# A decode step of cached attention and a gated feed-forward block: the TensorE program as a loop over four units

## The chip, the cores and the metric

The kernel runs on one core of a Trainium2 chip. The metric is the device time of one execution in microseconds (us); lower is better. Engines are called PE (TensorE), DVE (VectorE), ACT (ScalarE), POOL (GpSimd) and SP (SyncE, which here only issues DMAs).

## What is computed

One decode step for a batch of two, all in bfloat16 with D = 448:

```python
xn = layernorm(x)                                    # x: (2, 1, 448)
q = (xn @ wq).reshape(2, 1, 16, 256)                 # wq: (448, 4096)
k, v = last 2048 of 8192 cache positions, 8 heads    # each serves two query heads
o = softmax(q k^T / 16) v                            # per batch and head
s = o.reshape(2, 1, 4096) @ wo                       # wo: (4096, 448)
g = silu(relu(xn @ w1) @ w2)                         # w1: (448, 1792), w2: (1792, 448)
out = x + s * g
```

## The kernel before

The K and V that are read make 33.5 MB of the 44.1 MB that the kernel reads. They are cut into four units u = 0 to 3, each with one batch and four key heads (`divmod(u, 2)`), so that a unit's K or V is one tile of 128 partitions by 16384 values (32 KB in a partition, 4 MB in all). A load of such a tile is one DMA.

For each unit the work is a chain:

- `do_turn(u)`: DVE transposes the K tile in four pieces from a buffer `ub` into the one tile `kt`.
- `do_S(u)`: PE makes the scores in the PSUM bank `sbk`: four matmuls with `amask`, one for each column group (`tile_position`), that put a large negative number where a query does not belong to a key head, and then 32 matmuls with `qz`, the spread out queries.
- `do_chain(u)`: DVE takes the maximum `rm`, PE turns it into a row of `mbk`, DVE folds it into `m8` and `mrow`, PE turns it back (a float32 matmul with `one_f`), DVE copies it to `bias`, ACT computes the exponential `e_sb`, DVE transposes it into `ptd`, PE sorts it into the bank `pbk` with 16 matmuls, and ACT copies it into `pt[u % 2]`. `do_sum(u)` makes the reciprocal `rs` of the sum (PE `gsum`, DVE).
- `do_PV(u)`: 32 matmuls of `pt` with the V tile into `obk`.
- `do_o(u)`: DVE scales to `o_sb`, PE transposes it with four matmuls, DVE spreads it into `at_exp`.

The queries come first: `do_q_mm` multiplies the normalised x (`xr`) with wq, which lies in the tile `wqo` on 128 partitions as seven slots of half rows, into `obk`; `do_q` scales (`q_n`), transposes (`q_t`), spreads with four matmuls (`rep4`) and makes all eight pieces of `qz`. The feed-forward block is `do_H` (28 matmuls with w1 into `hbk`), `do_hT` and `do_F` (56 matmuls with w2 into `fbk`, then silu). At the end 128 matmuls with wo into the bank `wbk`, a product with g, a sum with x, and the store.

Buffers: `ub` has three tiles, and `place` says which load uses which: k0, k2 (after k0) and v2 in tile 0; k1, v1 and v3 in tile 1; v0 and k3 in tile 2. A K tile is free when its turn is over (`freed[f"k{u}"]`), a V tile when its `do_PV` is over. wo overwrites wq in `wqo`; w1 and w2 have tiles of their own.

`_Prog` records every operation with the operations that it depends on. Each engine gets its list in the order of recording; an operation that somebody needs counts up its engine's semaphore, every DMA has a semaphore of its own, and waits are for values of these counts. All of it is written out straight: no engine branches. All big loads are on SP, in the order wq (first slot), k0, wq (rest), k1, v0, k2, v1, k3, v2, w1, v3, w2, wo in four parts (`WO_PARTS`: 20, 8, 2 and 2 of its 32 slots), and then 15 small loads `probe` that nothing but SP's last wait needs. SP issues in order, so a load that waits for its buffer holds back the ones behind it. Matmuls have the helper's line L244 in the profile; loads have L36.

The order of PE in the second half of the recording:

```python
do_S(1); do_PV(0); do_o(0); do_chain(1); do_sum(1)
do_S(2); do_PV(1); do_chain(2); do_sum(2); do_o(1)
do_PV(2); do_S(3); do_H(); do_chain(3); do_sum(3); do_o(2)
do_PV(3); do_o(3)    # then the transposes of at_exp, do_F, wo
```

Of the kernel before, what the change touches and what calls it, by code (L numbers as in the profile page):

```python
# [5 lines left out]
BF = mybir.dt.bfloat16  # L6
# [8 lines left out]
class _Op:  # L15
    __slots__ = ("eng", "fn", "deps", "dma", "needed", "value", "sem")

    def __init__(self, eng, fn, deps, dma):
        self.eng, self.fn, self.deps, self.dma = eng, fn, deps, dma
        self.needed, self.value, self.sem = dma, 0, None  # L20


class _Prog:


    def __init__(self, nc, es):
        self.nc, self.es = nc, es
        self.lists = {PE: [], DVE: [], ACTE: [], SP: [], POOL: []}

    def op(self, eng, fn, deps=()):  # L30
        o = _Op(eng, fn, [d for d in deps if d is not None], False)
        self.lists[eng].append(o)
        return o

    def dma(self, eng, dst, src, deps=()):
        o = _Op(eng, lambda e: e.dma_start(dst, src), [d for d in deps if d is not None], True)  # L36
        self.lists[eng].append(o)
        return o

    def run(self):  # L40
        n = 0
        for ops in self.lists.values():
            for o in ops:
                for d in o.deps:
                    d.needed = True
        for e, ops in self.lists.items():
            sem, count = self.es.enter_context(self.nc.semaphore(f"s_{e}")), 0
            for o in ops:
                if o.dma:
                    n += 1  # L50
                    o.sem, o.value = self.es.enter_context(self.nc.semaphore(f"d_{n}")), 16
                elif o.needed:
                    count += 1
                    o.sem, o.value = sem, count

        def emit(eng, ops):
            seen = {}
            for o in ops:
                want = {}
                for d in o.deps:  # L60
                    if d.value > want.get(id(d.sem), (None, 0))[1]:
                        want[id(d.sem)] = (d.sem, d.value)
                for key, (sem, value) in want.items():
                    if value > seen.get(key, 0):
                        eng.wait_ge(sem, value)
                        seen[key] = value
                made = o.fn(eng) if o.fn else None
                if o.needed:
                    made.then_inc(o.sem, 16 if o.dma else 1)

        for name, e in (("sync", SP), ("scalar", ACTE), ("gpsimd", POOL), ("vector", DVE), ("tensor", PE)):
            emit(getattr(self.nc, name), self.lists[e])


def bass_recurrent_scan__sliding_block_cached__dense_activation_relu__decode_kernel(
# [25 lines left out]
    SLOTS = 7  # L101
    HC = HD // 2
    FC = DFF // 2
    WO_PARTS = [20, 8, 2, 2]
    NCOL = D // 4

    es = contextlib.ExitStack()
    with es:
# [5 lines left out]
        def psum(name, shape, dt):  # L114
            return es.enter_context(nc.psum_tensor(name, shape, dt))
# [7 lines left out]
        one_f = named("one_f", [128, 1], F32)  # L123
        par8 = named("par8", [128, 8], F32)
        par2 = named("par2", [128, 2], F32)
        qmask = named("qmask", [128, 4], F32)
        fold = named("fold", [128, 32], BF)
        gsum = named("gsum", [128, 128], F32)
        amask = named("amask", [128, 32], BF)
        x_sb = named("x_sb", [128, D], BF)  # L130
        xg = named("xg", [128, 9 * 128], BF)
# [4 lines left out]
        xr = named("xr", [128, SLOTS * 4], BF)  # L136
        q_n = named("q_n", [128, 512], BF)
        q_t = named("q_t", [128, 512], BF)
        rep4 = named("rep4", [128, 512], BF)
        m8 = named("m8", [1, 8], F32)  # L140
        qz = named("qz", [128, NU * 8 * 32], BF)
        fold8 = named("fold8", [128, 8], F32)
        xr2 = named("xr2", [128, SLOTS * 32], BF)
        h_n = named("h_n", [128, FC // 4], BF)
        h_t = named("h_t", [128, FC // 4], BF)
# [5 lines left out]
        probe = named("probe", [16, 16 * 15], BF)  # L151
        rm = named("rm", [128, 1], F32)
        mrow = named("mrow", [128, 128], F32)
# [5 lines left out]
        pt = [named(f"pt{i}", [128, 512], BF) for i in range(2)]  # L159
# [3 lines left out]
        wqo = named("wqo", [128, 32 * D], BF)  # L163
        assert SLOTS * HC <= 32 * D
        ub = [named(f"ub{i}", [128, UW], BF) for i in range(3)]
        kt = named("kt", [128, UW], BF)
        w1_sb = named("w1_sb", [128, SLOTS * FC], BF)
        w2_sb = named("w2_sb", [128, 14 * D], BF)

        sbk = psum("sbk", [128, 512], F32)  # L170
        pbk = psum("pbk", [128, 512], F32)
        obk = psum("obk", [128, 512], F32)
        fbk = psum("fbk", [128, 512], F32)
        wbk = psum("wbk", [128, 512], F32)
        mbk = psum("mbk", [128, 512], F32)
        hbk = psum("hbk", [128, 512], F32)

        def mbk_ap(lo, n, rows=128):
            return view(mbk, lo, [[1, n]], n=rows)

        def kv_src(u, cache):
            hg, b = divmod(u, 2)
            a = cache[b, 4 * hg:4 * hg + 4, SK - W:SK, :]
            return a.rearrange("h (p t) d -> p h (t d)", t=NT)
# [5 lines left out]

        wq_src = A_wq.rearrange("r (hf c) -> (r hf) c", hf=2).rearrange("(p s) c -> p (s c)", s=SLOTS)
        w1_src = B_w1.rearrange("r (hf c) -> (r hf) c", hf=2).rearrange("(p s) c -> p (s c)", s=SLOTS)
        w2_src = B_w2.rearrange("(hf p j) n -> p hf (j n)", hf=2, j=7)
# [5 lines left out]
            base=0, pattern=[[-1, 128]], channel_multiplier=1), [i0])  # L199
        i1 = pr.op(POOL, lambda e: e.memset(ident_f[:, :], 0.0), [p_id])  # L200
# [3 lines left out]
        p_one = pr.op(POOL, lambda e: e.memset(one_f[:, :], 1.0), [p_idf])  # L204
        p_at = pr.op(POOL, lambda e: e.memset(at2[:, :], 0.0))
        p_x2 = pr.op(POOL, lambda e: e.memset(xr2[:, :], 0.0))
# [7 lines left out]
        for e2 in range(2):  # L214
            v_xn = pr.op(DVE, lambda e, e2=e2: e.tensor_scalar(
                out=view(xg, 128 - 127 * e2, [[256, 4], [128, 2], [2, 64]], n=B),
                in0=view(x_sb, 3 * e2, [[1, 4], [0, 2], [SLOTS, 64]], n=B),
                scalar1=st2[0:B, 0:1], scalar2=rstd[0:B, 0:1],
                op0=ALU.subtract, op1=ALU.mult), [v_rs])
        v_par = pr.op(DVE, lambda e: e.tensor_reduce(  # L220
            out=par2[:, :], in_=view(ident, 0, [[1, 2], [2, 64]]), axis=AX.X, op=ALU.add), [p_id])
        v_par8 = pr.op(DVE, lambda e: e.tensor_copy(
            view(par8, 0, [[2, 4], [1, 2]]), view(par2, 0, [[0, 4], [1, 2]])), [v_par])
        v_qm = pr.op(DVE, lambda e: e.tensor_reduce(
            out=qmask[:, :], in_=view(ident, 0, [[32, 4], [1, 32]]), axis=AX.X, op=ALU.add))
# [5 lines left out]
        for i in range(4):  # L231
# [5 lines left out]
        v_gs = pr.op(DVE, lambda e: e.tensor_copy(  # L237
            view(gsum, 0, [[8, 16], [1, 8]]), view(fold8, 0, [[0, 16], [1, 8]])), [v_fold8])
        v_am = pr.op(DVE, lambda e: e.tensor_scalar(
            out=view(amask, 0, [[8, 4], [2, 4], [1, 2]]), in0=view(ident, 0, [[0, 4], [1, 4], [0, 2]]),  # L240
            scalar1=-1.0, scalar2=BIG, op0=ALU.add, op1=ALU.mult), [p_id])

# [4 lines left out]
        for s in range(SLOTS):  # L247
            m_xr = pr.op(PE, mm(mbk_ap(2 * s, 2), xg[0:B, 128 * s + 128:128 * s + 256], ident[0:B, 0:B], s == 0),
                         [v_xn, p_id])
        v_xr = pr.op(DVE, lambda e: e.tensor_tensor(  # L250
            out=view(xr, 0, [[4, SLOTS], [2, 2], [1, 2]]), in0=view(mbk, 0, [[2, SLOTS], [0, 2], [1, 2]]),
            in1=view(par8, 0, [[1, SLOTS], [1, 2], [0, 2]]), op=ALU.mult), [m_xr, v_par8])

        v_xr2 = pr.op(DVE, lambda e: e.tensor_copy(
            view(xr2, 0, [[32, SLOTS], [1, 2], [16, 2]]), view(xr, 0, [[4, SLOTS], [2, 2], [1, 2]])), [v_xr, p_x2])

        st = {"mbk": v_xr}
        dma_of, freed = {}, {}
        place = {"k0": 0, "k1": 1, "v0": 2, "k2": 0, "v1": 1, "k3": 2, "v2": 0, "v3": 1}
        last_in = {}  # L260

        def load(name):
            i, u = place[name], int(name[1])
            dma_of[name] = pr.dma(SP, ub[i][:, :], kv_src(u, A_k_cache if name[0] == "k" else A_v_cache),
                                  [freed.get(last_in.get(i))])
            last_in[i] = name

        def do_turn(u, g0=0, g1=4):
            src = ub[place[f"k{u}"]]
            s32, k32 = src[:, :].bitcast(F32), kt[:, :].bitcast(F32)  # L270
            for g in range(g0, g1):
                lo, hi = g * UW // 8, (g + 1) * UW // 8
                st["turn", u, g] = pr.op(DVE, lambda e, lo=lo, hi=hi: e.transpose(k32[:, lo:hi], s32[:, lo:hi]),  # L273
                                         [dma_of[f"k{u}"], st.get(("S", u - 1))])
            freed[f"k{u}"] = st["turn", u, g1 - 1]

        def do_q_mm(s0, s1):
            deps = [d_wq[s0 > 0], v_xr, st["obz"]]
            for s in range(s0, s1):
                for i in range(4):  # L280
# [233 lines left out]
```

## Time and profile before

| | |
|---|---|
| median of 3 runs | 111.34 us (111.20 to 111.41) |
| the profiled execution's own time | 111.39 us |
| its span, from the first to the last instruction | 109.9 us |
| mean granted clock of PE | 0.761 |
| busy PE, weight load (PEld), DVE, ACT, POOL | 41.1, 19.2, 58.0, 11.0, 2.5 us |
| read from HBM | 44.11 MB, 401 GB/s over the span |
| PE matmul records | 625 |

How to read the views that follow. The DMA line gives, in 40 equal slices of the span or of the window asked for, the mean busy share of the 16 DMA engines in tenths (9 is 90% or more). A queue line has packets, MB and the share of 16 engines' time; q1 is SP's queue, q10 that of ACT, and q8 and q14 carry instructions. The chain of waits in order of time has start, length and what it was. The timeline has start, length, engine, line, operation, tile written and tiles read, and in brackets how long the engine had been idle and what ended it. Times to landing are from the issue of a DMA to the moment when its semaphore is complete.

### The profile page before, as it was taken

To read this page: it belongs to the slowest core of one execution; us is meant where nothing else is said; L and a number is where in the kernel's file an instruction comes from. 1 tells how busy PE (TensorE), PEld (TensorE's weight loads), DVE (VectorE), ACT (ScalarE), POOL (GpSimd) and SP (SyncE) were. 2 spreads that over 40 slices of the span, in tenths; PEclk is the share of its full clock that TensorE was granted. 3 is DMA by queue.
4 is the path that set the end of the run, shared out by engine and by line. 5 is a ranking of instruction groups with operands and counts; after the bars stand their busy time and mean duration, and the time that the engine had idled before them with its cause. 6 is when DMAs were issued, how large, how long until landed. Compare 5 with 4: busy or idle time off the path is not lost.

```text
span 109.9 us, 1444 instructions
## 1 busy us (share of the span) xinstructions
PE 41.1 (37%) x625; PEld 19.2 (17%) x625; DVE 58.0 (53%) x85; ACT 11.0 (10%) x21; POOL 2.5 (2%) x12
## 2 busy tenths in 40 slices
PE   0120000275921302982310059620049913575281
PEld 0000000012211101321210024210013512213270
DVE  1870089937068697016389941348995245123401
ACT  2900000014011200000310000040000022000000
POOL 6200000000000000000000000000000000000000
PEclk9999999999995555599855556995555996569555
DMA  3989999998999899989999998999899988999930
GB/s 59 514 382 465 441 429 429 441 465 382 417 513 405 382 447 489 394 382 465 468 394 405 477 453 382 423 477 429 359 423 482 465 376 373 432 428 416 400 116 7
DMA packets 2706, 44.21 MB, mean 402 GB/s; under 512 B 522, under 2 KB 780, under 8 KB 1292
## 3 DMA queue, kind: packets, MB, share of 16 engines
q1 hardware_dynamic: 2672, 44.11, 94.4%
q8 instruction: 5, 0.08, 0.3%
q10 hardware_dynamic: 28, 0.01, 0.0%
q14 instruction: 1, 0.01, 0.0%
HBM read 44.11 MB, written 0.00 MB: 401 GB/s over the span
## 4 chain that ended last, share of the span: by engine, by line
DMA 49%; PE 22%; DVE 20%; issue 3%; SPq 2%; ACT 1%
DMA wqo<-in_A_wo_dram 31%; DMA wqo<-in_A_wq_dram 18%; DVE kt L273 14%; PE sbk L244 11%; PE obk L244 6%; PE mbk L244 2%; SPq L36 2%; PE wbk L244 1%; DVE ptd L334 1%; DVE rm L319 1%; PE pbk L244 1%; ACT e_sb L329 1%; PE mbk L321 1%; DVE o_sb L363 1%; ACT q_n L288 1%
## 5 line engine op out<-in xcount | busy, mean ns | idle before, releaser
L273 DVE STREAM_TRANSPOSE kt<-ub 128x2048 f32<-128x2048 f32 x16 | 35.6, 2279 | 6.4 <-DMA ub<-in_A_k_cache_dram 6.4
L244 PE MATMUL obk<-ub,pt 128*16 128x512 bf16 x128 | 11.0, 503 | 8.2 <-DMA ub<-in_A_v_cache_dram 8.2
L244 PE MATMUL sbk<-kt,qz 128*32 128x512 bf16 x128 | 12.6, 556 | 0.0
L244 PE MATMUL obk<-wqo,xr 128*4 128x512 bf16 x28 | 3.3, 619 | 15.4 <-DMA wqo<-in_A_wq_dram 13.4
L244 PE MATMUL sbk<-ident,amask 128*32 128x512 bf16 x16 | 2.4, 585 | 16.5 <-DVE kt L273 15.9
L363 DVE TENSOR_SCALAR o_sb<-obk,rs 128x512 bf16<-128x512 f32 x4 | 3.0, 742 | 10.3 <-PE obk L244 10.3
L329 ACT ACTIVATE e_sb<-sbk,bias 128x512 bf16<-128x512 f32 x4 | 2.7, 687 | 53.5 <-DVE bias L328 53.5
L319 DVE TENSOR_REDUCE rm<-sbk 128x1 f32<-128x512 f32 x4 | 2.8, 689 | 9.8 <-PE sbk L244 9.8
L244 PEld LDWEIGHTS obk<-ub,pt 128*16 128x16 bf16 x128 | 3.7, 108 | 14.0 <-DMA ub<-in_A_v_cache_dram 8.4
L244 PEld LDWEIGHTS sbk<-kt,qz 128*32 128x32 bf16 x128 | 4.6, 131 | 6.8 <-issue 6.1
L244 PE MATMUL pbk<-ptd,ident 128*32 128x128 bf16 x64 | 2.0, 264 | 8.5 <-DVE ptd L334 8.5
L244 PE MATMUL wbk<-wqo,at 128*17 128x112 bf16 x128 | 3.4, 296 | 3.0 <-DMA wqo<-in_A_wo_dram 3.0
L334 DVE STREAM_TRANSPOSE ptd<-e_sb 128x512 bf16<-128x512 bf16 x4 | 2.8, 702 | 2.5 <-ACT e_sb L329 2.5
L244 PEld LDWEIGHTS obk<-wqo,xr 128*4 128x4 bf16 x28 | 0.8, 108 | 17.2 <-DMA wqo<-in_A_wq_dram 13.9
L244 PEld LDWEIGHTS sbk<-ident,amask 128*32 128x32 bf16 x16 | 0.5, 113 | 17.1 <-DVE kt L273 16.4
L244 PEld LDWEIGHTS wbk<-wqo,at 128*17 128x17 bf16 x128 | 2.8, 131 | 3.5 <-DVE g_sb L406 2.8
L343 ACT ACTIVATE pt<-pbk 128x512 bf16<-128x512 f32 x4 | 2.4, 598 | 6.7 <-PE pbk L244 6.7
L349 DVE RECIPROCAL rs<-mbk 128x1 f32<-128x1 f32 x4 | 0.7, 169 | 4.1 <-PE mbk L244 4.1
L477 DVE TENSOR_TENSOR tmp<-wbk,g_sb 128x112 f32<-128x112 f32 x1 | 0.3, 274 | 4.7 <-PE wbk L244 4.7
L244 PEld LDWEIGHTS pbk<-ptd,ident 128*32 128x32 bf16 x64 | 1.2, 112 | 8.8 <-DVE ptd L334 8.8
L288 ACT ACTIVATE q_n<-obk 128x512 bf16<-128x512 f32 x1 | 0.6, 597 | 18.8 <-PE obk L244 18.8
L244 PE MATMUL mbk<-one_f,mrow 1*128 1x1 f32 x8 | 1.5, 256 | 2.5 <-DVE mrow L325 2.5
(66 smaller groups left out, 35.9 us busy)
## 6 DMA issues: line engine op xcount, KB each, us to landing
ub<-in_A_k_cache_dram SPq DMA_DIRECT2D x4, 4096.0 KB, 25.4
ub<-in_A_v_cache_dram SPq DMA_DIRECT2D x4, 4096.0 KB, 21.4
w_sb<-in_B_w_dram SPq DMA_DIRECT2D x2, 1568.0 KB, 23.8
wqo<-in_A_wq_dram SPq DMA_DIRECT2D x1, 3072.0 KB, 19.5
wqo<-in_A_wo_dram SPq DMA_DIRECT2D x1, 2240.0 KB, 32.6
wqo<-in_A_wo_dram SPq DMA_DIRECT2D x1, 896.0 KB, 34.5
wqo<-in_A_wq_dram SPq DMA_DIRECT2D x1, 512.0 KB, 3.7
wqo<-in_A_wo_dram SPq DMA_DIRECT2D x2, 224.0 KB, 34.5
```

Of the source, the lines that this page charges most:

```text
L36: o = _Op(eng, lambda e: e.dma_start(dst, src), [d for d in deps if d is not None], True)
L244: return lambda e: e.matmul(out_ap, lhsT=lhsT, rhs=rhs, start=start, stop=stop, skip_group_check=True, **kw)
L273: st["turn", u, g] = pr.op(DVE, lambda e, lo=lo, hi=hi: e.transpose(k32[:, lo:hi], s32[:, lo:hi]), [dma_of[f"k{u}"], st.get(("S", u - 1))])
L288: a = pr.op(ACTE, lambda e: e.activation(q_n[:, :], obk[:, :], ACT.Copy, scale=SCALE), [st["q_mm"], st["obz"]])
L319: v = pr.op(DVE, lambda e: e.tensor_reduce(out=rm[:, :], in_=sbk[:, :], axis=AX.X, op=ALU.max), [st["S", u]])
L321: m = pr.op(PE, lambda e: e.matmul(mbk_ap(0, 128, 1), lhsT=rm[:, :], rhs=ident_f[:, :], start=True, stop=True, is_transpose=True), [v, p_i ...
L329: a = st["exp", u] = pr.op(ACTE, lambda e: e.activation(e_sb[:, :], sbk[:, :], ACT.Exp, bias=bias[:, 0:1], accum_out=ssum[:, 0:1]), [v, st ...
L334: t = st["ptd", u] = pr.op(DVE, lambda e: e.transpose(ptd[:, :], e_sb[:, :]), [a, st.get(("sp", u - 1))])
L343: st["pt", u] = pr.op(ACTE, lambda e: e.activation(pt[u % 2][:, :], pbk[:, :], ACT.Copy), [o, st.get(("PV", u - 2))])
L349: st["rs", u] = st["mbk"] = pr.op(DVE, lambda e: e.reciprocal(rs[:, u:u + 1], mbk_ap(130, 1)), [st["gs", u]])
L363: st["osb", u] = pr.op(DVE, lambda e: e.tensor_scalar(out=o_sb[:, :], in0=obk[:, :], scalar1=rs[:, u:u + 1], scalar2=None, op0=ALU.mult), ...
L477: v_t = pr.op(DVE, lambda e: e.tensor_tensor(out=tmp[:, :], in0=wbk[:, 0:NCOL], in1=g_sb[:, :], op=ALU.mult), [m_o, st["g"]])
```

## The change

- PE's program for the units is stored once, as a loop of four turns (`Fori`). A turn is S(u), the transposes of o for u − 1, the chain of u, in the last turn alone H, and PV(u). In the turns PE does not wait for counts but takes credits: each producer (`gives`) adds to a semaphore of its own, and PE waits for the amount and takes it off again (`takes`). What comes ahead of the loop and behind it stays straight.
- Two buffers hold K (u % 2), one holds V. V2 and V3 are loaded in two halves, each when the same half of the PV before is done; PV waits for `va` at its start and for `vb` in its middle. K(u) waits for S(u − 2) instead of the turn of u − 2.
- wq and w1 lie on 112 partitions (`XP`) as four slots of whole rows instead of 128 partitions with seven slots of half rows. q is computed with 32 matmuls into two banks, H with 16 of 448 columns instead of 28 of 224. w1 is in the end of `wqo`, so that wo's later parts wait for H.
- The mask is written by one matmul over 128 columns of weights instead of four.
- `qz` is one tile for one unit, made again for each unit ahead of its turn; the maximum goes back by a transpose; w2 lies as 14 rows in a partition; the transposes of o have a bank of their own (`tbk`); the 15 small loads `probe` are gone.

The core of the diff:

```diff
+        with nc.tensor.Fori(0, len(self.turns)) as i:
+            a, _, b = self.turns[0]
+            emit(nc.tensor, a, {})
+            with nc.tensor.If(i == len(self.turns) - 1):
+                emit(nc.tensor, self.turns[-1][1], {})
+            emit(nc.tensor, b, {})
+        emit(nc.tensor, self.tail, seen)
...
+                for name, amount in o.takes:
+                    eng.wait_ge(self.credit[name], amount)
+                    eng.sem_inc(self.credit[name], -amount)
...
-        wq_src = A_wq.rearrange("r (hf c) -> (r hf) c", hf=2).rearrange("(p s) c -> p (s c)", s=SLOTS)
-        w1_src = B_w1.rearrange("r (hf c) -> (r hf) c", hf=2).rearrange("(p s) c -> p (s c)", s=SLOTS)
-        w2_src = B_w2.rearrange("(hf p j) n -> p hf (j n)", hf=2, j=7)
+        wq_src = A_wq.rearrange("(p s) c -> p (s c)", s=NS)          # NS = 4, XP = D // NS = 112
+        w1_src = B_w1.rearrange("(p s) c -> p (s c)", s=NS)
+        w2_src = B_w2.rearrange("(p j) n -> p (j n)", j=NF)
...
+        def load_k(u):
+            k_in[u] = pr.dma(SP, ub[u % 2][:, :], kv_src(u, A_k_cache), [st.get(("S", u - 2))])
+
+        def load_v(u):
+            free = st.get(("PV", u - 1, 0)), st.get(("PV", u - 1, 1))
+            if u < 2:
+                pr.dma(SP, ub[2][:, :], kv_src(u, A_v_cache), free, gives=("va", 16))
+            else:
+                for half, name in enumerate(("va", "vb")):
+                    lo = half * UW // 2
+                    pr.dma(SP, ub[2][:, lo:lo + UW // 2], kv_src(u, A_v_cache, half * NT // 2, (half + 1) * NT // 2),
+                           [free[half]], gives=(name, 16))
...
+        def pe_S(u):
+            pr.op(PE, mm(sbk[:, :], amask[:, :], view(ident, 0, [[0, 128], [1, 4]]), True), takes=[("kt", 1)])
+            for wp in range(8):
+                for g in range(4):
+                    st["S", u] = pr.op(PE, mm(sbk[32 * g:32 * g + 32, :], view(qz, 32 * wp, [[1, 32]]), ...
...
+        d_wq = [pr.dma(SP, wqo[0:XP, 0:HD], wq_src[:, 0:HD])]
+        load_k(0)
+        d_wq.append(pr.dma(SP, wqo[0:XP, HD:NS * HD], wq_src[:, HD:NS * HD]))
+        load_k(1)
+        load_v(0)
+        do_turn(0)
+        do_q_mm(0, 1)
+        do_q_mm(1, NS)
+        do_q()
+        for u in range(NU):
+            pr.turn()
+            pr.within(0)
+            pe_S(u)
+            pe_oT(u - 1)
+            pe_chain(u)
+            pr.within(1)
+            if u == NU - 1:
+                pe_H()
+            pr.within(2)
+            pe_PV(u)
+            if u == 0:
+                do_qz(0, True)
+                load_k(2)
+                load_v(1)
+                dve_chain(0, lambda: do_turn(1, 0, 1))
+                do_qz(1)
+                do_turn(1, 1, 4, True)
+            else:
+                if u > 1:
+                    do_qz(u)
+                    do_turn(u, gives=True)
+                dve_osb(u - 1)
+                dve_chain(u)
+                if u == 1:
+                    load_k(3)
+                    load_v(2)
+                    d_w1 = pr.dma(SP, wqo[0:XP, W1_AT:W1_AT + NS * DFF], w1_src, [st["q_mm"]])
+                if u == 2:
+                    load_v(3)
+        pr.after()
+        d_w2 = pr.dma(SP, w2_sb[:, :], w2_src)
+        for n in WO_PARTS:
+            d_wo.append((j0, pr.dma(SP, wqo[:, j0 * D:(j0 + n) * D], wo_src[:, j0 * D:(j0 + n) * D],
+                                    [st["q_mm"], st["H"] if j0 else None])))
...
-        d_probe = [pr.dma(SP, probe[0:k, 16 * (k - 1):16 * k], A_x[0, 0, 0:16 * k].rearrange("(k c) -> k c", c=16))
-                   for k in range(1, 16)]
-        pr.op(SP, None, d_probe)
```

## The prediction

> **What bounds the kernel now.** First the page's DMA lines. They show a stream that hardly pauses: from the second slice to the 38th the engines are 0.8 to 0.9 busy or more, and nearly all bytes are on one queue.
>
> ```profile
> DMA  3989999998999899989999998999899988999930
> q1 hardware_dynamic: 2672, 44.11, 94.4%
> q8 instruction: 5, 0.08, 0.3%
> ```
>
> Rate of one engine: 44.11 MB / (0.944 × 109.9 us × 16) = 26.6 KB/us (KB of 1000 here). The stream alone needs 44.11 MB / 16 / 26.6 = 103.6 us. Queue q8 fetched instructions: five packets of 16 KB, 0.3% × 109.9 × 16 / 5 = 1.06 us each, each on one engine.
>
> Next the chain of waits in order of time: its end is the landing of wo, then 1.38 us of matmuls.
>
> ```profile
> 71.64 34.53 DMA wqo<-in_A_wo_dram
> 106.16 0.04 issue
> 106.21 1.38 PE wbk L244 x48
> 107.61 0.28 DVE tmp L477
> ```
>
> Then the DMA view cut to 103.0 to 109.9 us, 40 slices of 0.17 us. All engines work until 104.9; then only 0.3 of them, some four or five of 16, until 105.9, 0.2 until 106.3, 0.1 until 106.65.
>
> ```profile
> DMA  9989898998953333322110000400000000000000
> q8 instruction: 2, 0.03, 2.0%
> ```
>
> So the end is set by stragglers: engines that finish 0.9 to 1.65 us after the rest. Shared out, their work (2.1 slice-shares × 0.17) is 0.36 us; all would end at 105.3. The DMA view cut to 38 to 40, 68 to 72 and 88 to 91 us shows one q8 packet in each, and the tail two more: three ahead of four or five stragglers. That a fetch makes its engine a straggler is my reading of it.
>
> Compute is covered. The timeline at the last unit: PE waits for v3 until 94.57, and the 80 wbk matmuls wait for wo until 103.84, while F ended at 101.2.
>
> ```profile
> 94.57 3.59 PE L244 MATMUL obk<-ub,pt 128*16 128x512 bf16 x32 [1.94 <-DMA ub<-in_A_v_cache_dram]
> 103.84 2.05 PE L244 MATMUL wbk<-wqo,at 128*17 128x112 bf16 x80 [2.68 <-DMA wqo<-in_A_wo_dram]
> ```
>
> **The loads' order, and whether the queue runs dry.** SP issues in order; what is issued late costs only if the engines have emptied their queues. Landings now (issue plus the DMA view's time to landing): v0 42.1, k2 51.8, v1 61.5, k3 71.5, v2 81.1, w1 84.8, v3 94.5, w2 98.3, wo 103.7 to 107. A queue is empty about 1 us ahead of its last landing.
> - k2 now waits for S(0) instead of turn(0): issued at some 31 instead of 23.0; the queue holds v0 until 41. Cover 10 us.
> - v1 waits for PV(0), which now stands ahead of S(1): v0 lands at 42.1, 3.6 us of matmuls (the row of 94.57), issued at 45.7 instead of 43.4, with k2 in the queue until 50.8. Cover 5 us. k3 queues behind it and for S(1), about 51; v1 lasts until 60.5.
> - v2 in halves waits for the halves of PV(1), 63.3 and 65.1; k3 lasts until 70.5. v3 in halves for PV(2): 78.3 and 82.9; w1 lasts until 83.8, the first half until 88.7.
> - wo after its first 2240 KB waits for H, now in the last turn, at about 95.3; the first part lasts until 102.7. Cover 7 us.
> No load starves. Four half loads for two whole ones add two issues of 0.54 us on an idle SP; Their 16 KB rows lie between the 32 KB rows of the window 50 to 76 us (424 GB/s) and the 12.25 KB rows of 79.3 to 82.2 (402 GB/s): 0 to 5% of 19.5 us, 0 to 1.0; I take 0.1, near the 32 KB rows, as the short window's value is coarse (96 packets). Below nothing is excluded: no transfer gets shorter rows and fewer bytes. The 15 probes leave: they stand after wo, and the 15.4 us that SP waits for them releases nobody. Cost 0.
>
> **wq and w1 on 112 partitions.** Now 128 rows of 4 + 24 KB and of 12.25 KB; then 112 rows of 8 + 24 KB and of 14 KB. The bytes are the same. Lower bound 0: 7 rows for each of 16 engines. Upper bound: rows go where they go now, 8 to a lane (128/16), so 14 lanes carry 8 longer rows: 8 × 4 KB = 32.8 thousand bytes for wq, 8 × 1.75 KB = 14.3 for w1, at 26.6 KB/us 1.23 + 0.54 = 1.77 us. A lane that is late stays late, since nothing evens it out before wo. I take the upper bound: every big row of this trace is a 128-row transfer with eight rows to a lane.
>
> [...] No transfer of this trace has 112 partitions.
>
> At the start the first piece of wq is 896 KB instead of 512, so k0 lands 393 thousand bytes / 16 / 26.6 = 0.92 us later, and turn(0) with it; then q_t has twice the columns (0.45 us more), the two qz operations ahead of S(0) replace two of eight (0), half of q_n goes to DVE (0.4 us beside ACT's 0.6). S(0) starts some 1 to 2 us later than 26.29, with the 10 us of cover above.
>
> **The PE program as a loop.** Stored matmuls fall from 625 to about 335; with a weight load each, 1250 records against 670. Five fetches for 1250 are 250 records a fetch, so 670 need 2.7. What the loop's three returns fetch again isn't in this trace. Bounds: nothing (fetches fall by two), or two blocks at each return, since the loop of some 210 records need not lie in one block (fetches rise to about nine). For the stragglers: with two fewer the worst that is left may be 0.9 to 1.3 late in place of 1.65, a gain of 0.35 to 0.75; with nine, spread over engines as now, none. I take −0.3.
>
> [...]
>
> A return stands after PV(u) and ahead of S(u+1). A fetch that stalls it costs at least the 1.06 us of its packet and at most the 3.7 us from issue to landing of the first wq transfer. Covers: at the first return, DVE's turn(1) until 44.4 and PV(0) until 45.7 (dispatch runs ahead of the matmuls); at the last, turn(3) until about 85.3 against PV(2)'s end at 82.9. Credits add seven waits with a decrement to each turn, not in the trace; the chain's "issue" pieces of 0.02 to 0.05 us each give 0.14 to 0.35 us a turn.
>
> **The compute path to the end.** qz leaves the first turn: 0.21 × 2 = 0.42 us a turn on DVE, ahead of each turn(u); o_sb (0.75) moves ahead of the maximum, beside S. The max column by one transpose instead of two passes saves about 0.1; the mask by one matmul of 0.58 in place of four side by side in 0.62 is 0. Adding up from v0: S(1) 45.7 to 48, turn(2) to 64 to 66, S(2) 65 to 67, turn(3) to 85.3, S(3) to 89.5, chain 4.8 to 94.3, H to 95.3, PV(3) to 98.9 (98.2 now), o_sb to at 1.9, F and what follows 0.9: PE is ready for wbk at about 102, and wo's first part lands at 103.7 or later. Cover 1.7 us; past it each us of stall costs one.
>
> **The sum.** Against the profiled run's 111.39 us (span 109.9, 1.49 around it; the median of three is 111.34): rows +1.77, halves +0.1, stragglers −0.3, the rest hidden: 112.96, rounded to 112.9.
>
> **Rivals.**
> 1. Balanced rows, stragglers as now: the 112 rows make no late lane and the loop fetches as much as it saves. 111.4. For it: 112 divides by 16, and bytes are equal.
> 2. Faster: the tail of stragglers shrinks. Place: 105.3 to 106.65 us, where 0.1 to 0.3 of the engines work. Price: up to 1.35 us if all end together; 109.9 to 111.1, say 110.3. It decides if rows are balanced and fewer than about three fetches fall before wo. For it: stored records nearly halve. Against: a loop may fetch more.
> 3. Slower still: returns stall PE past the 1.7 us of cover, in the turns' chain S, maximum, turn, S. Three returns of 3.7 us and a second block each make up to 11 to 22 us less the covers (5 + 2 + 2): 114 to 118. Against: dispatch runs ahead, and PE idles 9 us before S(2) now.
> 4. That the change does not do what it says is part of 1: a program half as long that fetches as often.
>
> **How the numbers follow.** A difference of 0.2% (0.22 us) is about what a measurement of this kernel can tell. Forecast 112.9 (112.0 to 113.7) 0.56; rival 1 0.15; rival 2 0.17; rival 3 0.12. Rival 1 gives 0.10 to no change, 0.03 to faster, 0.02 to slower. Faster 0.20, same 0.10, slower 0.70. The range reaches into rival 2 to 110.5 and into rival 3 to 114.2. The forecast's own range is 112.0 to 113.7.
>
> **What would show it.** In the DMA view's last microseconds: right, if more than half of the engines (digits of 5 or more) work on past 105.5 and wo's first landing moves from 103.8 to 105 or later; wrong, if the drop to 0.3 stays at 105. q8 packets: 3 against 8 or more tells whether the loop fetches again. The loop is on the path if the 80 wbk matmuls wait for DVE or for issue, not for wo; a queue ran dry if a slice between 10 and 100 us falls below 0.7.

## The result and the profile after

| | before | after |
|---|---|---|
| median of 6 runs each | 111.45 us (111.20 to 112.77) | 120.33 us (119.41 to 121.59) |
| profiled execution: time, span | 111.39, 109.9 us | 121.59, 120.1 us |
| mean granted clock of PE | 0.761 | 0.786 |
| PE matmul records | 625 | 602 |

The changed kernel is slower by a ratio of 1.0756 [1.0686, 1.0826], that is 8.9 us by the medians. The prediction was 112.9 us, in a range of 110.5 to 114.2: the sign is right, the size is not. Its profiled execution is the longest of its six, some 1.3 us longer than a median run and 10.2 us longer than the profiled execution of before.

The page of after: the DMA engines' busy share, what they moved, and the queues.

```profile
DMA  4989899999999999999989898999998999999910
GB/s 91 390 382 491 357 319 237 319 306 415 458 415 426 447 404 464 404 458 393 480 382 472 382 469 382 420 426 431 280 237 231 398 431 428 423 440 411 362 44 1
q1 hardware_dynamic: 2544, 44.11, 93.9%
q8 instruction: 2, 0.03, 0.1%
```

The same GB/s line of before, in slices of 2.75 us instead of 3.0:

```profile
GB/s 59 514 382 465 441 429 429 441 465 382 417 513 405 382 447 489 394 382 465 468 394 405 477 453 382 423 477 429 359 423 482 465 376 373 432 428 416 400 116 7
```

No slice of after shows a dry queue: the engines are as busy as before (93.9% against 94.4%), over a span that is 10 us longer, with the same 44.11 MB. So they were busy with slower work. Where, the GB/s line says: slices 5 to 9 (12 to 27 us) move 237 to 357 GB/s, and slices 29 to 31 (84 to 93 us) 231 to 280, where before, between its first slice and its end, never falls under 359. These are the times of wq and of w1. Against the 428 GB/s of after's slices 10 to 28, each slice loses (1 − rate/428) × 3.0 us: 4.2 us in the five at wq and 3.8 in the three at w1, 8.0 of the 10.2 by which this execution is longer. Of the rest some 1.3 us lie in the last three slices, and most of what is left in the first four.

The DMA view cut to the time of wq's long transfer, after (15.1 to 24.6 us) and then before (13.6 to 20.3 us):

```profile
DMA packets 122, 2.68 MB, mean 282 GB/s; under 512 B 13, under 2 KB 13, under 8 KB 13
```

```profile
DMA packets 116, 2.80 MB, mean 418 GB/s; under 512 B 2, under 2 KB 2, under 8 KB 2
```

And at w1, after (83.9 to 90 us) and then before (79.3 to 82.2 us):

```profile
DMA packets 126, 1.61 MB, mean 264 GB/s; under 512 B 15, under 2 KB 15, under 8 KB 15
```

```profile
DMA packets 96, 1.17 MB, mean 402 GB/s; under 512 B 3, under 2 KB 3, under 8 KB 3
```

The trace's records of single packets give the same per row, as means: a 24 KB row of wq took 0.91 us before and 1.43 after, a row of w1 0.47 us for 12.25 KB before and 0.93 us for 14 KB after. The rows of K and V that move at the same time slow down with them. Over the whole run a 32 KB row takes 1.24 us in place of 1.22, but those that overlap the loading of wq take 1.33 (before 1.21), and the 16 KB rows of V that overlap w1 take 0.84 (0.62 in the first kernel below, which has the old layout). Summed over a run and divided by 16 engines, the rows of wq take 13.2 us after against 9.1 before, those of w1 6.5 against 3.8, and those of K and V 80.4 against 77.9. So about a quarter of the added time stands in the neighbours' rows.

The chain of waits in order of time (start, length, what) and PE's timeline of after:

```profile
91.14 22.91 DMA wqo<-in_A_wo_dram
...
114.19 2.05 PE wbk L273 x70
...
116.28 1.50 PE wbk L273 x38
```

```profile
27.19 0.61 PE L273 MATMUL obk<-wqo,xr 112*17 112x512 bf16 x4 [19.51 <-DMA wqo<-in_A_wq_dram]
...
67.25 3.59 PE L273 MATMUL obk<-ub,pt 128*16 128x512 bf16 x32 [9.12 <-PEq L97]
70.77 0.61 PE L273 MATMUL sbk<-ident,amask 128*128 128x512 bf16 x1
...
114.19 3.57 PE L273 MATMUL wbk<-wqo,at 128*17 128x112 bf16 x128 [4.00 <-DMA wqo<-in_A_wo_dram]
```

The end is bound as before by the landing of wo; it has moved from 103.84 to 114.19 us. The queries wait for wq until 27.19, so over half of the delay is there before the loop begins. Before, it was 21.41:

```profile
21.41 2.73 PE L244 MATMUL obk<-wqo,xr 128*4 128x512 bf16 x24 [13.39 <-DMA wqo<-in_A_wq_dram]
```

The loop itself shows no stall: at the return into S(2) the mask's matmul starts at 70.77, as PV(1) ends. "PEq L97" is PE's wait for a credit.

### The profile page after: what moved, and what is told of

Its sections match the earlier page's. It is cut to its first block, busy times and chain, and to the rows that moved or that the text cites. A ratio compares the mean times of both kernels' runs of the same rounds, so it can differ in the third digit from the quotient of the medians.

```text
span 120.1 us, 1419 instructions
## 1 busy us (share of the span) xinstructions
PE 46.3 (39%) x602; PEld 18.9 (16%) x602; DVE 58.2 (48%) x82; ACT 10.6 (9%) x20; POOL 2.3 (2%) x12
## 3 DMA queue, kind: packets, MB, share of 16 engines
q1 hardware_dynamic: 2544, 44.11, 93.9%
HBM read 44.11 MB, written 0.00 MB: 367 GB/s over the span
## 5 line engine op out<-in xcount | busy, mean ns | idle before, releaser
L273 PE MATMUL obk<-ub,pt 128*16 128x512 bf16 x128 | 14.7, 625 | 23.2 <-PEq L97 23.2
L273 PE MATMUL sbk<-kt,qz 128*32 128x512 bf16 x128 | 11.1, 502 | 0.0
L273 PE MATMUL obk<-wqo,xr 112*17 112x512 bf16 x16 | 2.5, 615 | 21.3 <-DMA wqo<-in_A_wq_dram 21.3
L273 PEld LDWEIGHTS sbk<-kt,qz 128*32 128x32 bf16 x128 | 3.7, 115 | 6.7 <-issue 5.4
L273 PE MATMUL hbk<-wqo,xr 112*17 112x512 bf16 (+1 forms) x32 | 4.2, 601 | 0.0
L273 PEld LDWEIGHTS obk<-wqo,xr 112*17 112x17 bf16 x16 | 0.5, 116 | 22.8 <-DMA wqo<-in_A_wq_dram 22.3
L324 DVE TENSOR_SCALAR q_n<-hbk 128x512 bf16<-128x512 f32 x1 | 0.7, 690 | 4.6 <-PE hbk L273 4.6
L273 PE MATMUL sbk<-ident,amask 128*128 128x512 bf16 x4 | 2.4, 596 | 1.2 <-PEq L97 1.2
```

The costliest lines, as they stand in the source:

```text
L273: return lambda e: e.matmul(out_ap, lhsT=lhsT, rhs=rhs, start=start, stop=stop, skip_group_check=True, **kw)
L324: v = pr.op(DVE, lambda e: e.tensor_scalar(out=view(q_n, 256, [[512, 2], [1, 256]]), in0=view(hbk, 0, [[256, 2], [1, 256]]), scalar1=SCALE ...
```

## The experiments

Two theories at the start. Rows: the transfers to 112 partitions are slow, and nothing else in the change costs. Loop: the loop, its credits or the single V buffer delay the loads.

**Rows undone, and the loop undone too.** The first kernel is after with wq and w1 back on 128 partitions, in seven slots of half rows (w1 still in `wqo`, behind wo's first 20 slots; w2 in the old form too). The second has in addition the four turns written out.

```diff
-        wq_src = A_wq.rearrange("(p s) c -> p (s c)", s=NS)
-        w1_src = B_w1.rearrange("(p s) c -> p (s c)", s=NS)
+        wq_src = A_wq.rearrange("r (hf c) -> (r hf) c", hf=2).rearrange("(p s) c -> p (s c)", s=SLOTS)
+        w1_src = B_w1.rearrange("r (hf c) -> (r hf) c", hf=2).rearrange("(p s) c -> p (s c)", s=SLOTS)
```

```diff
-        with nc.tensor.Fori(0, len(self.turns)) as i:
-            a, _, b = self.turns[0]
+        for k, (a, h, b) in enumerate(self.turns):
             emit(nc.tensor, a, {})
-            with nc.tensor.If(i == len(self.turns) - 1):
-                emit(nc.tensor, self.turns[-1][1], {})
+            if k == len(self.turns) - 1:
+                emit(nc.tensor, h, {})
             emit(nc.tensor, b, {})
```

Expected of the first:

> The kernel after, with wq and w1 back on 128 partitions as seven slots of half rows (28 matmuls for q into one bank, 28 for H); the loop, the credits, the one V buffer, the halves and the mask stay. Theory of the rows (all 16 engines are slowed while they move 112-row transfers; the trace after has 24 KB rows at some 1.4 us where the trace before has 0.91): most of the loss goes, 111.4 to 112.8 us, and the slices of wq and w1 come back from 240-320 to over 380 GB/s. Theory of the loop (returns and credits hold PE, the loads start late): it stays at 119 to 121. Theory of the buffers (one V buffer, two K buffers: the queue runs dry): 119 to 121 too, with slices below 0.7 between the loads.

Expected of the second:

> As a_128, with the four turns written out one after the other; credits as in the loop. Only the returns go, and the instructions are fetched in a row. Theory that a fetch of instructions makes a straggler among the DMA engines: q8 packets rise from 2 to 5, and it is 0.3 to 1.2 us slower than a_128. Theory that the loop's returns cost PE: it is 0.3 us or more faster than a_128. Theory that neither reaches the path: within 0.3 us.

Measured: with the rows undone 111.61 us (111.08 to 112.61, 12 runs), 0.9976 [0.9938, 1.0014] of before; with the loop undone too 111.42 (111.19 to 112.46, 12 runs), 0.9965 [0.993, 1.0]. The page of the first has no hole at wq or w1 any more:

```profile
GB/s 69 505 383 490 410 430 439 466 442 383 407 526 407 383 425 490 419 383 442 478 419 386 454 454 419 371 436 425 431 423 432 436 425 395 427 456 424 380 143 7
...
q8 instruction: 3, 0.05, 0.2%
```

and the page of the second, straight one fetches more:

```profile
q8 instruction: 5, 0.08, 0.3%
```

So all of the loss is undone with the rows. What remains of the change (loop, credits, two K buffers and one for V, halves, mask, one unit's `qz`, w1 in `wqo`) costs nothing and brings nothing that these runs can separate from zero. The loop saves two of five fetches, and no time. The tail fits that, in the DMA view from 101 to 108 us in slices of 0.175 us; first with the loop, then straight:

```profile
DMA  4848999799799696999798331111111000000003
```

```profile
DMA  9288979894986999799899453332222000004000
```

With the loop the tail is thinner (0.1, some two or three engines, against 0.2 to 0.5) but ends at the same 106.4 us: two or three late engines held wo's last part as long as three to eight.

**One transfer of the two.** After with wq alone on 128 partitions; w1 stays on 112, w2 in its new form.

> The kernel after with only wq on 128 partitions; w1 stays on 112. Theory of the rows: w1 keeps its 6.3 us in place of 3.7, so it is 2.2 to 3.0 us slower than a_128, and some 5 us faster than after. My first sizing (only the lanes with eight rows are late, 0.54 us for w1): 0.5 us slower than a_128. Theories of the loop or of the buffers: as after, 119 to 121.

Measured: 115.9 us (114.81 to 117.2), 1.0318 [1.0259, 1.0377]. Its page, of its longest run (117.2 us), has the second hole alone:

```profile
GB/s 88 456 488 408 422 434 408 470 442 374 510 397 442 442 368 499 408 351 476 408 445 442 374 453 408 419 431 328 244 213 281 431 419 419 448 415 412 348 50 1
```

By the medians w1 costs 115.9 − 111.6 = 4.3 us, and what is left for wq is 120.3 − 115.9 = 4.4; wq alone on 112 partitions was not run. The 4.3 is more than the 2.2 to 3.0 that I had expected, and the packet records say why: w1's own rows take 6.8 us of every engine in place of 3.8, about as expected, but V's 16 KB rows take another 1.3 us more than with the rows undone (21.0 against 19.7).

**The rows alone.** Before with the rows of after for wq, w1 and w2, with the matmuls of q and H that go with them, and everything else as it was: PE's program straight, three shared buffers, whole loads, w1 in a tile of its own.

```diff
-        wq_src = A_wq.rearrange("r (hf c) -> (r hf) c", hf=2).rearrange("(p s) c -> p (s c)", s=SLOTS)
-        w1_src = B_w1.rearrange("r (hf c) -> (r hf) c", hf=2).rearrange("(p s) c -> p (s c)", s=SLOTS)
+        wq_src = A_wq.rearrange("(p s) c -> p (s c)", s=NS)
+        w1_src = B_w1.rearrange("(p s) c -> p (s c)", s=NS)
```

> The kernel before with wq and w1 on 112 partitions as after has them (q in two banks, H with 16 matmuls, w2 as 14 rows in a partition); no loop, three buffers with the old places, whole V loads, the old mask. Theory of the rows: it loses nearly all that after loses, 118 to 120.5 us. Theories of the loop or of the buffers: 111 to 112. My first sizing: 113.

Measured: 120.86 us (120.14 to 122.19), 1.0773 [1.071, 1.0837]: the whole of the loss (a little over the 118 to 120.5 expected) without any other part of the change. Both holes are on its page:

```profile
GB/s 88 395 472 405 416 288 263 296 348 362 515 362 493 384 460 411 427 449 416 460 375 482 362 515 362 499 362 416 233 230 245 312 488 362 407 436 443 375 165 1
```

**Why 112 rows are slow.** Three theories: the source (whole DRAM rows read differently from half rows), the count (seven rows for an engine), or the partitions (a transfer that reaches fewer than 128 of them moves slower for that alone; a guess of mine at this point). Before, with wq and w1 in their old layout on 128 partitions, source rows and row lengths unchanged, but each transfer cut by partition: into 0 to 63 and 64 to 127, or into 0 to 111 and 112 to 127.

```diff
-        d_wq = [pr.dma(SP, wqo[:, 0:HC], wq_src[:, 0:HC])]
+        CUT = ((0, 64), (64, 128))           # the other kernel: ((0, 112), (112, 128))
+        d_wq = [[pr.dma(SP, wqo[a:b, 0:HC], wq_src[a:b, 0:HC]) for a, b in CUT]]
...
-        st["w1"] = pr.dma(SP, w1_sb[:, :], w1_src)
+        st["w1"] = [pr.dma(SP, w1_sb[a:b, :], w1_src[a:b, :]) for a, b in CUT]
```

Expected of the cut at 64:

> The kernel before; the three transfers of wq and w1 are each cut into two DMAs, partitions 0 to 63 and 64 to 127. Same bytes, rows, row lengths, sources and places. [...] Theory of the source (the new row lengths or pitches in HBM made the 112-row transfers slow): nothing changes, 111 to 112. Theory of the count (seven rows for an engine is a bad number): nothing changes, there are four.

Expected of the cut at 112:

> As b_cut64, cut into partitions 0 to 111 and 112 to 127. [...] Theory of the source: 111 to 112, since rows and pitches are those of before. Theory of the count: the 112-row pieces alone pay, 4 to 7 us more.

Measured: cut at 64, four runs from 128.69 to 134.39 us, median 132.44; cut at 112, four runs from 125.04 to 128.15, median 127.16; before beside them 111.44. They scatter more than the runs of the other kernels, so the losses below are taken from their lowest times; pages and rows are those of the profiled executions, of 130.87 and 126.17 us. The pages, cut at 64 and then at 112:

```profile
GB/s 92 325 486 334 352 182 243 182 182 205 415 395 425 476 395 420 466 405 425 466 387 436 466 395 436 461 385 411 133 182 223 277 410 425 348 441 438 387 145 6
```

```profile
GB/s 93 308 420 410 394 252 221 252 221 163 389 441 420 420 452 410 436 431 431 420 434 463 389 463 399 447 420 441 285 237 271 300 415 422 367 453 433 378 172 6
```

The holes are back, deeper, at the same two places. The source as I put it is refuted: rows and pitches are those of before. So is the count: a half has four rows for an engine, fewer than seven, and is the slowest; a 24 KB row took 1.94 us (median) in it against 0.91 uncut. What is left of the three is which partitions a transfer reaches. But the cut at 64 lost more than its own rows account for: half the rate for wq and w1 is 12.4 us (an estimate from the rate of before, 5.28 MB / 16 / 26.6 KB/us), and it lost at least 17. The packet records show where the rest is. With the cut at 64 the rows of wq and w1 take 13.4 us more of every engine than before (26.3 against 12.9), near the 12.4, and the rows of K and V 5.0 more (83.0 against 77.9); with the cut at 112 it is 9.5 and 4.3. The 12.4 leaves the neighbours out.

**Are 32 neighbours slower than 64?** The same with four pieces of 32 partitions, `CUT = ((0, 32), (32, 64), (64, 96), (96, 128))`.

> As b_cut64, in four pieces of 32 partitions. [...] If the rate goes by the share of the partitions, the rows take twice as long again, near 3.8 us, and it is 145 us or more.

Measured: 126.62 and 129.19 us, against 128.69 to 134.39 with the cut at 64, and a 24 KB row took 1.92 us (median, in the run of 126.62 us), as in the pieces of 64.

```profile
GB/s 91 360 388 482 322 236 173 220 236 291 388 492 367 482 388 445 461 377 492 369 471 398 440 471 372 482 377 471 196 192 273 219 445 408 374 436 440 400 201 6
```

So a row in a piece of 32 neighbouring partitions took as long as in a piece of 64, and both about twice as long as in the transfer to all 128 (1.92 and 1.94 us against 0.91). The 32 that the piece of 64 has in addition brought no rate here, and a rate by the share of the partitions, near 3.8 us a row, is refuted. What makes it so is not shown.

Cutting as such is not what slows the rows: here there are twice as many transfers as with the cut at 64 and the rows are no slower, and V cut by columns, all 128 partitions in each half, takes 0.615 us for a 16 KB row where 32 KB take 1.22 (in the kernel with rows undone). But a cut by partition also changes how many rows an engine has and which rows of DRAM are read together. A piece of 64 partitions that are not neighbours has as many rows as the half, so it would help to tell these apart; it was not run.

**The halves of V.** After with the rows undone, and V2 and V3 loaded whole, when all of the PV before is done; PV no longer waits for `vb`.

```diff
-            if u < 2:
-                pr.dma(SP, ub[2][:, :], kv_src(u, A_v_cache), free, gives=("va", 16))
-            else:
-                for half, name in enumerate(("va", "vb")):
...
+            pr.dma(SP, ub[2][:, :], kv_src(u, A_v_cache), [st.get(("PV", u - 1, 1))], gives=("va", 16))
```

> As a_128, with V2 and V3 loaded whole. If one V buffer is covered only because of the halves: PV(2) waits for all of v2 (81.1) and v3 is issued at about 84.8, when the queue's w1 has ended at 83.8, so the DMA engines run dry for 1 to 2 us and the time rises by as much: 112.5 to 113.5. If the halves are not needed: within 0.3 us of a_128.

Measured: 115.45 us (115.17 to 115.88), 1.0364 [1.0329, 1.0398], 3.8 us above the same kernel with halves, and more than I had expected. The page (slices of 2.85 us), SP's timeline and two windows of 1 us (busy PE, PEld, DVE, ACT, POOL, granted clock, DMA share, GB/s):

```profile
GB/s 71 482 415 506 348 466 449 394 483 437 368 518 403 385 506 391 403 506 380 414 486 380 449 472 368 460 449 355 401 26 357 380 368 421 425 482 409 379 110 1
```

```profile
84.80 0.54 SPq L42 DMA_DIRECT2D ub<-in_A_v_cache_dram  x1
```

```profile
84.00:85.00 1.00, 1.00 (x9) 0.10 (x1) 0.19 (x1) 0.00 (x0) 0.00 (x0) 0.50 0.00 0
85.00:86.00 1.00, 1.00 (x9) 0.29 (x12) 0.56 (x1) 0.00 (x0) 0.00 (x0) 0.52 0.00 0
```

V3 is issued at 84.80, as PV(2) ends, and the queue has nothing: no byte from 84 to 86 us, 26 GB/s in that slice. This is what a dry queue looks like, and no other kernel here shows it. Against 420 GB/s the slices 30 to 33 lose 2.7 + 0.4 + 0.3 + 0.4 = 3.8 us. The single V buffer is free only because it is released in halves.

Its tail, from 104 to 111 us, tells something of the stragglers:

```profile
DMA  0994099209979979999996799999900000000000
```

After the dry spell the engines run in step (the share swings between 0 and 0.9 until 105.2), and the one fetch on q8 since 38.8 us comes at 108.9: the share falls from 0.9 to 0 in one slice, without the 1.5 us of single engines at the end of the other kernels. That fits my reading that fetches make stragglers. It does not prove it, since the dry spell has levelled every other difference as well.

**A warmer PE at the end.** The last 128 matmuls of before run at half the clock (granted 0.5 from 103 to 108 us, 27 ns each). Before with 10 matmuls of no use behind F, into `pbk`, so that PE does not stand still ahead of wo:

```diff
         do_F()
+        for _ in range(10):
+            pr.op(PE, mm(pbk[:, :], ident[:, :], ptd[:, :], True, True))
```

> The kernel before with ten matmuls of 512 columns into the idle bank pbk between F and the wo matmuls; their result is not used. The wbk matmuls run at half the clock (granted 0.5 from 102 to 108 us), and 48 of them, 1.38 us, stand behind the last big landing. If PE stays at full clock: these 48 take 0.7 to 0.9 us and the time falls by 0.4 to 0.7 us. If PE falls to half clock anyway: the ten take 4.3 us, end at about 105.6, and it is 0 to 1 us slower.

Measured: 111.79 us (111.20 to 113.48, 12 runs), 1.0000 [0.9967, 1.0033]. The timeline:

```profile
102.41 3.89 PE L244 MATMUL pbk<-ptd,ident 128*128 128x512 bf16 x9 [0.33 <-issue]
106.23 1.75 PE L244 MATMUL wbk<-wqo,at 128*17 128x112 bf16 x128
```

The wo matmuls take 1.75 us, 14 ns each (granted clock 1.0 from 106 to 108 us), instead of 3.4, but the useless ones run until 106.2, over 2 us after wo's first part lands in before (103.84). In after with the rows undone F ends earlier, at 99.3, so there is room for them; the same with 16 there:

> As a_128, with sixteen matmuls of 512 columns into the idle bank pbk after F, where the clock is still full (granted 1.0 from 98 to 100 us) and PE then waits 4.4 us for wo; their result is not used. If they hold the clock: they end at about 103, the 128 wbk matmuls take 2 instead of 3.5 us, and the end moves from the last matmul to the last landing of wo (106.9): 0.2 to 0.6 us faster than a_128, and faster than before. If the clock falls anyway: they take 6.8 us, wbk starts at 106.2, and it is 0.5 to 2 us slower than a_128.

Measured: 111.28 us (111.10 to 112.18, 12 runs), 0.9974 [0.994, 1.0007].

```profile
100.02 4.35 PE L290 MATMUL pbk<-ptd,ident 128*128 128x512 bf16 x15 [0.33 <-issue]
104.30 1.16 PE L290 MATMUL wbk<-wqo,at 128*17 128x112 bf16 x80
106.08 0.92 PE L290 MATMUL wbk<-wqo,at 128*17 128x112 bf16 x40 [0.62 <-DMA wqo<-in_A_wo_dram]
107.22 0.28 PE L290 MATMUL wbk<-wqo,at 128*17 128x112 bf16 x8 [0.21 <-DMA wqo<-in_A_wo_dram]
```

And without them:

```profile
103.77 3.49 PE L290 MATMUL wbk<-wqo,at 128*17 128x112 bf16 x128 [4.43 <-DMA wqo<-in_A_wo_dram]
```

With the useless matmuls wo's 128 no longer run at half clock (14.5 ns each in the first 80), as hoped, but the gain of 0.2 to 0.6 us does not come: against the runs of before beside it (median 111.80) the kernel stands at 0.9974, and without them at 0.9976 (of 112.11). Now PE waits for each part of wo and ends at 107.50; without them it went through all 128 to 107.26 with no wait in between. Two limits lie within 0.3 us of each other at this end: the matmuls at half clock, and the last straggler. Taking away one leaves the other. No kernel of this study beats before by more than its measurement is uncertain.

## Why the prediction was right or wrong, step by step

- **The bound.** Right. The landing of wo sets the end in every kernel here, and the DMA stream stays busy all along, but for the dry spell with V2 and V3 whole.
- **The loads' order.** Right, and closely, where the rows do not blur it. In the kernel with rows undone v1 is issued at 45.94 us (45.7 predicted), the halves of v3 when PV(2) frees them at 78.3 and 83.0 (78.3 and 82.9), S(1) starts at 45.82 (45.7 to 48), S(2) at 65.27 (65 to 67), S(3) at 82.92 (earlier than the 85.3 predicted), and H is done at 93.4 (95.3). No queue runs dry. The cost of the halves, put at 0.1, is not to be told from 0; the price of leaving them out is 3.8 us.
- **Rows of wq and w1: the step that failed.** I bounded it by 0 and 1.77 us and took the upper end; it measured 8.7 (4.4 + 4.3). The direction was right, and these rows are the reason, but the upper end was no bound. It counted eight longer rows to a lane, each at the old rate of 26.6 KB/us; that 112 rows go eight to a lane was my assumption, and no run shows it. That every engine keeps this rate the trace of before can show only for 128 rows. The packet records refute it: 24 KB rows of the same length got 1.57 times as long, and w1's rows 1.95 times for 1.14 times the bytes. And the sum has no term at all for the rows of K and V that move beside them, which pay about a quarter. A wider estimate, half the rate for both, would have been 12.4 us; nothing in before showed it, the cut at 64 then did (1.94 us for a 24 KB row against 0.91). With it the range would have reached some 123.5, and 120.3 lies within. It is no strict bound either, since the cut at 64 lost more. (The sum that was made, 112.96, rounds to 113.0, not 112.9; nothing hangs on it.)
- **The loop's fetches.** The count was right: 2.7 predicted, two or three measured, five when written out. The time was wrong: I took −0.3 us, and no gain is measured. The tail with the loop still ends at 106.4, and PE at half clock is as late; that fits, and no run separates the two.
- **The loop's returns.** That a return would have to wait for a fetch was an assumption. No run here shows such a wait: with three returns q8 has fewer packets than without (two or three against five), and in after S(2) starts at 70.77 us as PV(1) ends; with rows undone S(1), S(2) and S(3) start at 45.82, 65.27 and 82.92 us, as the PV before each ends. That dispatch runs ahead of the matmuls, before shows by half a microsecond: the weight loads of PV(0) end at 48.60, its matmuls at 49.09. PE's waits for credits lie in the time that the loads need anyway.
- **The compute path to the end.** Covered, by more than I had put: F ends at 99.3 us with rows undone, 4.4 us before wo lands, against a cover of 1.7.
- **The rivals.** Balanced rows, and faster, are refuted by the rows. The slower rival (114 to 118) lies nearest to the result, but by a mechanism that is not there: no return stalls PE. Its range did not follow from its own sum either: 11 to 22 us less 9 of cover is 113.5 to 124.6, and that 120.3 lies in there is chance.
- **What would show it.** Two signs stood as written: more than half of the engines worked on past 105.5 us, and wo's first landing came after 105, at 114.1. Any slowing of the stream would have set them off, so they do not show the mechanism. I had looked for the loss in a tail of late lanes; it lies at the transfers themselves, where all 16 engines are slow, and the GB/s line by slices shows it at once.

Open: why the rows are slower than sharing explains. Eight rows to the fullest lane, where seven would be even, is 8/7 = 1.14 times as long (an estimate), and per byte 1.57 (wq) and 1.71 (w1) were measured. Why the neighbours' rows slow down too is open as well; single 32 KB rows took up to 3.4 us with the cut at 64 and up to 3.9 with the cut at 112. Which engine wrote which partition is not in these traces.

## What to carry to other kernels

A transfer whose rows divide evenly by the DMA engines (112 / 16 = 7) is not yet as fast as one to 128 partitions: here 112 instead of 128 cost a factor of 1.6 to 1.7 per byte, and 64 or 32 a factor of 2.1, in a stream that was the bound. When a layout changes the number of partitions of a large load, let the range of the prediction reach that far, count in slower rows of the loads beside it (1.33 us against 1.21 for 32 KB), and look at the GB/s line of the page slice by slice, since the busy share does not show it. Here a buffer was given up for nothing because its release is cut into halves (111.61 us, 115.45 without them), and a cut in one of two limits that lie within 0.3 us of each other brought nothing (0.9974 of before against 0.9976).

## What the runs showed of the hardware

- Rows of a 112-partition load (means): 24 KB in 1.43 us against 0.91 for 128 partitions, 14 KB of w1 in 0.93 against 0.47 for 12.25 KB; in pieces of 64 and of 32 partitions 1.94 and 1.92 us for 24 KB (medians).
- Rows of 128-partition loads that moved at the same time slowed down too: 16 KB rows of V beside w1 0.84 us against 0.62, 32 KB rows of K and V beside wq 1.33 against 1.21.
- The busy share of the engines stayed at 0.94 while their rate fell to 231 to 357 GB/s in the slices of wq and w1: a slow packet counts as busy.
- PE went through a loop of four turns with two (after) or three (rows undone) fetches on q8 in the whole run, against five when written out, and with rows undone S(1), S(2) and S(3) started at 45.82, 65.27 and 82.92 us, as the PV before each ended.
- In the warmed kernels the granted clock rose from 0.5 to 1.0 at 106.0 us (before, 5.4 us after F began) and at about 101.9 (after with rows undone, 3.6 us after F began; the weight loads of the useless matmuls go from one in 0.43 us to nine in 1.82). A wo matmul then took 14 ns, and 27 ns in the kernels whose clock was 0.5 there.
